# Key additions on GpSimd, tied behind the work of their own steps

## The chip, the cores and the metric

The kernel runs on one core of a Trainium2 chip. The core has five engines that run side by side and wait for each other through semaphores: TensorE (PE in the profile) multiplies matrices and writes PSUM, VectorE (DVE), ScalarE (ACT) and GpSimd (POOL) work element by element, and SyncE (SP) issues the transfers between HBM and SBUF. Each engine does its own instructions strictly in order. The metric is the device time of one execution in microseconds (us); the time before is 1137.61 us, the median of three runs (1135.73, 1138.26, 1137.61).

## What is computed

Four batches of 12480 queries attend to 49 agents, which themselves attend to 12480 keys; each output row then goes through a two-layer network with `h * cos(h)` between its layers. Cut to what matters:

```python
def sm(a, b):
    s = scale * (a @ b.transpose(0, 2, 1))
    s = s - s.max(-1, keepdims=True)
    e = np.exp(s)
    return e / (e.sum(-1, keepdims=True) + 1e-09)

agent_v = sm(agents, k) @ v            # keys: 4 x 49 x 12480
attn = sm(q, agents) @ agent_v         # queries: 4 x 12480 x 49
h = attn.reshape(49920, 128) @ w_in    # 49920 x 2048
out = (h * np.cos(h)) @ w_out          # 49920 x 128
```

## The kernel before

**The main loop.** The 49920 queries are cut into 52 groups of 960 (13 a batch, `NG`), and a group into 16 steps (`STEP`): two halves of 480 queries times eight pairs of 128 hidden units. A step `n` does three things. `first_product` (L1038) multiplies a piece of `a` (agent values already times `w_in`) by the turned query weights `pT` into a PSUM pair `ph`; ACT takes the cosine of it (`c`, L1041); `cubic_part` on DVE forms `r` from `c` and `ph` (L1047). `second_product` (L1063), four steps behind (`LAG`), multiplies `r` by `w_out`. There are 832 steps.

**The queries.** For each group the scores go through PE and are copied to a tile `e`; DVE takes the maximum (`mx`, L663) and POOL subtracts it (L665, in the burst L720). Exponentials run for whole pieces of six or seven groups at once, since ACT must change its table for them (`query_exp`, L727). Then POOL sums the exponentials of each group by a tree of additions (`query_sum`, lines L738 to L742, seven instructions a group), DVE inverts the sums (`query_inverse`, L746, L747), and for each group in turn, ten steps ahead of its use, POOL forms the weights `p` (`query_weights`, L751), PE turns them (L760), ACT copies them (L764) and POOL writes `pT` in two casts and two subtractions (`query_turned`, L767, L768).

**The keys.** While the queries of batch b - 1 are worked off, the 13 key groups of batch b are scored into a large tile `s` (`Later.scores`, L523 to L530), shifted by their maximum on POOL (`shift`, L555), exponentiated in one instruction (`exp`, L558), multiplied with the values (`values`, L492, summed on DVE at L574 and L576), and added up group by group into `es` by 12 additions on POOL (`add`, L563, one of them short). DVE reduces `es` (`total`, L581), and PE and DVE make the normalisation of it (`inverse`, L587 to L590). The first batch has another way and no such additions. Tile `s` has one buffer; its next use begins with a memset on POOL (L514).

**The burst.** Once a batch, at step 97 of its 208, `burst` puts the exponentials of the first query piece, of the keys and of the second query piece behind one another on ACT, with one change of table. There are such bursts for key batches 1, 2 and 3, at about 203, 473 and 743 us, and a last one without keys. The seven sums of the first query piece follow in the next steps; those of the second piece are planned from 16 steps behind the burst on (`lazy_sum`, L899), in a `kept_behind`.

**The order of the work.** The program is written step by step; `Plan` collects for each step which small work goes with it. The key addition of group g is planned at `plan(at + 44 + 3 * g, ab[b].add, g)` (L998), 47 to 80 steps behind the start of the burst. But what each engine really does in which order is decided by a scheduler, which may move an instruction ahead of others on its engine where no dependency forbids it. Two helpers add such dependencies, without any wait at run time: `as_traced` keeps all instructions of a stretch in their written order, and `kept_behind(engines)` ties each instruction written inside it behind the last one written before it on the same engine. It doesn't tie what comes after.

Of the kernel before, what the change touches and what calls it, by code (L numbers as in the profile page):

```python
# [46 lines left out]
def agent_attention_cos_ffn(ctx, tc, qT, kT, v, vk, vk_rest, agT, w_in, w_out, outT):  # L47
    nc = tc.nc
# [70 lines left out]
    @contextmanager  # L119
    def kept_behind(engines):  # L120

        traced = nc.cur_bb.bb.instructions
        start = len(traced)
        last = {}
        for i in reversed(traced):
            if i.engine in engines and i.engine not in last:
                last[i.engine] = i
            if len(last) == len(engines):
                break
        yield  # L130
        for i in list(traced[start:]):
            if i.engine in engines:
                tc.add_manual_dep(i, last[i.engine].name, mybir.DependencyInfo(mybir.DependencyClass.NoSync,
                                  mybir.DependencyReason.DATA), reason="kept_behind")
                last[i.engine] = i
# [121 lines left out]
    class Agents:  # L257
# [51 lines left out]
        def add(self, g):  # L309

            if g == 0:
                nc.gpsimd.tensor_copy(self.es, self.part(0))
            else:
                nc.gpsimd.tensor_add(self.es, self.es, self.part(g))
# [191 lines left out]
    class Later(First):  # L506
# [53 lines left out]
        def add(self, g):  # L560
            s = self.s[:, 8 * g:min(8 * g + 8, NT_K)]
            es = self.es[:, :s.shape[1]]
            nc.gpsimd.tensor_add(es, self.s[:, :8] if g == 1 else es, s)  # L563

        def values(self, g):
            e = self.part(g)
# [698 lines left out]
```

## Time and profile before

| | |
|---|---|
| time, median of 3 runs | 1137.61 us (1135.73 to 1138.26) |
| the profiled execution | 1132.91 us, of which 1131.0 us span |
| PE, DVE, ACT, POOL busy | 93%, 90%, 85%, 39% of the span |
| additions of the keys' exponentials, L563 | 36 on POOL |
| granted clock of TensorE, mean | 0.971 of full speed |

The page gives each engine's busy time, the chain of work that ended last with its shares by engine and line, and the costliest groups of instructions. The timeline has one line for each run of like instructions in order of time: start, length, engine, line, operation, names of the tiles written and read, count, and in brackets the idle time before it and what ended it. The table of waits adds these up by pairs of lines. POOL's share is small as a mean over the span, and its work is uneven: POOL is busy for 31.32 of the 35 us from 205 to 240 us.

### The profile page before, as it was taken

What the parts mean: (1) busy time and instruction counts of PE and PEld (TensorE: products, weight loads), DVE (VectorE), ACT (ScalarE), POOL (GpSimd) and SP (SyncE); (2) the same over time, 40 slices, a digit from 0 to 9 for tenths busy, and PEclk for the clock granted to TensorE, in tenths of its full rate; (3) what the DMA queues carried; (4) which work ended last, traced back from release to release, by engine and by line L of the source; (5) the groups of instructions that cost most, each with busy time, mean ns of one, the idle gap of its engine ahead of it and who ended that gap; (6) DMA issues with size and microseconds to landing.
All of it is one profiled execution on the core that took longest, in us unless ns stands there. A gap on an engine that the chain in (4) does not pass through costs nothing.

```text
span 1131.0 us, 30442 instructions
## 1 busy us (share of the span) xinstructions
PE 1047.6 (93%) x12759; PEld 800.4 (71%) x12759; DVE 1021.0 (90%) x1144; ACT 958.5 (85%) x1239; POOL 440.0 (39%) x733
## 2 busy tenths in 40 slices
PE   6888999869999999869999999986999999989997
PEld 2666777657877787657787777765777777766775
DVE  5859999769999999958998999986999999999997
ACT  4768888958889999868888999895898999999996
POOL 2022336784222323797313231589422223162320
PEclk9899999889999999989999999998999999989999
DMA  9733465512112245432111234441100000000001
GB/s 369 284 116 113 147 199 199 181 56 73 40 38 92 74 128 185 143 111 78 53 55 37 89 95 162 151 147 37 59 37 19 36 18 36 36 18 33 20 36 38
DMA packets 32562, 108.58 MB, mean 96 GB/s; under 512 B 3616, under 2 KB 4896, under 8 KB 32416
## 3 DMA queue, kind: packets, MB, share of 16 engines
q1 hardware_dynamic: 32416, 106.55, 27.6%
q8 instruction: 102, 1.67, 0.6%
q14 instruction: 44, 0.36, 0.1%
HBM read 80.97 MB, written 25.56 MB: 94 GB/s over the span
## 4 chain that ended last, share of the span: by engine, by line
PE 46%; DVE 30%; POOL 12%; ACT 7%; issue 4%; DMA 0%; SPq 0%; ACTq 0%; POOLq 0%; DVEq 0%
DVE r L1047 26%; PE ph L1038 19%; PE one L1063 16%; ACT c L1041 4%; POOL s L555 3%; POOL es L563 3%; POOL tree L738 3%; PE one L492 2%; PE one L523 1%; PE one L169 1%; PE one L1059 1%; PE one L1060 1%; PE ph L492 1%; PE one L760 1%; ACT e L727 1%
## 5 line engine op out<-in xcount | busy, mean ns | idle before, releaser
L1047 DVE SCALAR_TENSOR_TENSOR r<-c,ph 128x960 fp32r<-128x960 f32 x832 | 909.2, 1148 | 60.7 <-ACT c L1041 58.4
L1041 ACT ACTIVATE c<-ph 128x960 f32<-128x960 f32 x832 | 790.2, 980 | 128.6 <-PE ph L1038 105.6
L1038 PE MATMUL ph<-pT,a 113*128 113x480 f32 x1664 | 538.3, 404 | 44.1 <-POOL pT L768 29.2
L1063 PE MATMUL one<-r,w 128*128 128x480 f32 x1664 | 505.3, 390 | 0.9 <-issue 0.5
L1038 PEld LDWEIGHTS ph<-pT,a 113*128 113x128 f32 x1664 | 288.4, 190 | 167.5 <-DVE r L1047 75.2
L1063 PEld LDWEIGHTS one<-r,w 128*128 128x128 f32 x1664 | 310.8, 191 | 51.4 <-DVE r L1047 1.4
L751 POOL TENSOR_TENSOR p<-e,rz 126x392 f32<-126x392 f32 x51 | 43.1, 847 | 386.1 <-PE one L760 334.5
L768 POOL TENSOR_TENSOR pT<-p,pT 49x480 fp32r<-49x480 f32 x102 | 124.5, 1221 | 7.8
L767 POOL CAST pT<-p 49x480 fp32r<-49x480 f32 x102 | 59.4, 582 | 61.9 <-ACT p L764 57.1
L665 POOL TENSOR_TENSOR e<-e,mx 126x392 f32<-126x392 f32 x43 | 36.4, 846 | 94.7 <-DVE mx L663 94.1
L1070 ACT COPY osb<-one 128x480 f32<-128x480 f32 x80 | 44.4, 555 | 2.3 <-PE one L1063 2.2
L492 PEld LDWEIGHTS one<-s,vt 128*32 128x32 f32 (+1 forms) x2352 | 31.8, 117 | 20.3 <-issue 11.1
L169 PEld LDWEIGHTS one<-ag,xt 128*32 128x32 f32 x2752 | 33.5, 110 | 16.8 <-issue 15.1
L492 PE MATMUL one<-s,vt 128*32 128x49 f32 (+1 forms) x2352 | 37.8, 218 | 8.0 <-ACT s L558 6.8
L738 POOL TENSOR_TENSOR tree<-tree 126x96 f32<-126x96 f32 x132 | 40.1, 304 | 8.6
L169 PE MATMUL one<-ag,xt 128*32 128x49 f32 x2752 | 39.7, 210 | 2.3 <-issue 2.3
L555 POOL TENSOR_TENSOR s<-s,mxb 128x392 f32<-128x392 f32 (+1 forms) x39 | 34.4, 927 | 17.1 <-DVE mxb L551 17.1
L1059 PE MATMUL one<-pT,b 113*128 113x480 f32 x104 | 40.5, 389 | 0.0
L1060 PE MATMUL one<-pT,b 113*128 113x480 f32 x104 | 39.8, 383 | 0.0
L523 PEld LDWEIGHTS one<-ag,xt 128*32 128x32 f32 x2340 | 28.4, 110 | 15.2 <-issue 7.7
L523 PE MATMUL one<-ag,xt 128*32 128x49 f32 x2340 | 33.8, 209 | 1.9 <-DVE s L527 1.9
L563 POOL TENSOR_TENSOR es<-es,s 128x392 f32<-128x392 f32 (+1 forms) x33 | 32.4, 982 | 0.0
(160 smaller groups left out, 643.5 us busy)
## 6 DMA issues: line engine op xcount, KB each, us to landing
outT<-osb SPq DMA_DIRECT2D x51, 480.0 KB, 2.7
xt<-qT SPq DMA_DIRECT2D x49, 480.0 KB, 4.0
xt<-kT SPq DMA_DIRECT2D x43, 512.0 KB, 3.7
vt<-vk SPq DMA_DIRECT2D x42, 512.0 KB, 4.5
c<-kT SPq DMA_DIRECT2D x5, 512.0 KB, 7.6
vt<-w_in SPq DMA_DIRECT2D x8, 256.0 KB, 6.9
vt<-w_out SPq DMA_DIRECT2D x8, 256.0 KB, 7.5
c<-vk SPq DMA_DIRECT2D x3, 512.0 KB, 7.4
```

What stands on the lines that cost most here:

```text
L169: mm = nc.tensor.matmul(out[at:at + n], xt[:, t * TT + lo:t * TT + lo + n], ag, start=True, stop=True)
L492: mm = nc.tensor.matmul(po[rows], vt[:, x, rows], e, start=(first and x == 0), stop=(last and x + 1 == len(es)))
L523: mm = nc.tensor.matmul(ps[j * QS:(j + 1) * QS, t], xt[:, t * w + j * QS:t * w + (j + 1) * QS], ag[:, self.b, :], start=True, stop=True)
L555: nc.gpsimd.tensor_sub(s, s, self.mxb.unsqueeze(1).to_broadcast(list(s.shape)))
L563: nc.gpsimd.tensor_add(es, self.s[:, :8] if g == 1 else es, s)
L738: nc.gpsimd.tensor_add(t[:, :, :w], src[:, :, :w], src[:, :, w:2 * w])
L767: nc.gpsimd.tensor_copy(pT[own, c], p[own])
L768: nc.gpsimd.tensor_sub(pT[other, c], p[own], pT[own, c].bitcast(F32))
L1038: nc.tensor.matmul(ph[:, j, :CH], ai[:, f], pTs[q % 3][:, c], start=True, stop=True)
L1041: nc.scalar.activation(cos, h, AF.Sin, bias=HALF_PI, scale=1.0)
L1047: nc.vector.scalar_tensor_tensor(r, cos, 1.0, h, op0=ALU.subtract, op1=ALU.mult)
L1063: nc.tensor.matmul(po, w1[:, f, :], r[:, j, :], start=(f == 0), stop=(f == NF - 1))
```

## The change

Each key addition is now written inside a `kept_behind` for GpSimd, so that the scheduler can't move it ahead of what was written before it on that engine.

```diff
         def add(self, g):
             s = self.s[:, 8 * g:min(8 * g + 8, NT_K)]
             es = self.es[:, :s.shape[1]]
-            nc.gpsimd.tensor_add(es, self.s[:, :8] if g == 1 else es, s)
+            with kept_behind([nc.gpsimd.engine]):
+                nc.gpsimd.tensor_add(es, self.s[:, :8] if g == 1 else es, s)
```

The order of the other engines stays the same. Lines behind L563 have a number higher by one in the changed program. In the order before, POOL's rows at the end of the fourth and in the fifth sum of the first burst read so (`tree` and `rz2` are the sums of the queries, `es` and `s` those of the keys):

```order
95 L738 TENSOR_TENSOR tree_3552<-tree_3552 126x8x6
96 L563 TENSOR_TENSOR es_1489<-s_1487 128x392
97 L738 TENSOR_TENSOR tree_3552<-tree_3552 126x8x3
98 L563 TENSOR_TENSOR es_1489<-es_1489,s_1487 128x392
99 L740 TENSOR_TENSOR rz2_1785<-tree_3552 126x8
100 L563 TENSOR_TENSOR es_1489<-es_1489,s_1487 128x392
101 L741 TENSOR_TENSOR rz2_1785<-rz2_1785,tree_3552 126x8
102 L563 TENSOR_TENSOR es_1489<-es_1489,s_1487 128x392
103 L742 TENSOR_TENSOR rz2_1785<-rz2_1785,e_1784 126x8
104 L738 TENSOR_TENSOR tree_3560<-e_1784 126x192
105 L563 TENSOR_TENSOR es_1489<-es_1489,s_1487 128x392
```

The additions stand one by one between the steps of the sums, twelve of them from the fourth sum to the sixth. In the order of the change the same place reads:

```order
95 L739 TENSOR_TENSOR tree_3552<-tree_3552 126x8x6
96 L739 TENSOR_TENSOR tree_3552<-tree_3552 126x8x3
97 L741 TENSOR_TENSOR rz2_1785<-tree_3552 126x8
98 L742 TENSOR_TENSOR rz2_1785<-rz2_1785,tree_3552 126x8
99 L743 TENSOR_TENSOR rz2_1785<-rz2_1785,e_1784 126x8
100 L739 TENSOR_TENSOR tree_3560<-e_1784 126x192
```

The sums follow one another with nothing between them. The additions stand further on, in the order of the change, on POOL between the query groups that come some 40 to 80 steps behind the burst (`p` are weights, `pT` the turned ones, `e` with `mx2` a query subtraction):

```order
174 L666 TENSOR_TENSOR e_3321<-e_3321,mx2_4303 126x392
175 L564 TENSOR_TENSOR es_1489<-s_1487 128x392
176 L564 TENSOR_TENSOR es_1489<-es_1489,s_1487 128x392 x2
177 L752 TENSOR_TENSOR p_0_104<-e_1784,rz2_1785 126x2x4x49
178 L768 CAST pT_1_99<-p_4465 49x480 x2
179 L769 TENSOR_TENSOR pT_1_99<-p_4465,pT_1_99 49x480 x2
180 L564 TENSOR_TENSOR es_1489<-es_1489,s_1487 128x392 x6
181 L752 TENSOR_TENSOR p_1_105<-e_1784,rz2_1785 126x2x4x49
182 L768 CAST pT_2_100<-p_4745 49x480 x2
183 L769 TENSOR_TENSOR pT_2_100<-p_4745,pT_2_100 49x480 x2
184 L564 TENSOR_TENSOR es_1489<-es_1489,s_1487 128x392
185 L666 TENSOR_TENSOR e_3321<-e_3321,mx2_4828 126x392
```

Two more follow behind that, ahead of the memset of `s`. In the order before, the same weights, casts and subtractions stand there without the additions. The second batch has the same pattern; the third has three, six and three additions, each lot behind a `pT`.

## Rows read from the trace of the kernel before

**Rows 1.** The page: busy time by engine; the chain's shares, by engine and line.

```profile
PE 1047.6 (93%) x12759; PEld 800.4 (71%) x12759; DVE 1021.0 (90%) x1144; ACT 958.5 (85%) x1239; POOL 440.0 (39%) x733
...
PE 46%; DVE 30%; POOL 12%; ACT 7%; issue 4%; DMA 0%; SPq 0%; ACTq 0%; POOLq 0%; DVEq 0%
DVE r L1047 26%; PE ph L1038 19%; PE one L1063 16%; ACT c L1041 4%; POOL s L555 3%; POOL es L563 3%; POOL tree L738 3%; PE one L492 2%; PE one L523 1%; PE one L169 1%; PE one L1059 1%; PE one L1060 1%; PE ph L492 1%; PE one L760 1%; ACT e L727 1%
```

**Rows 2.** Who waited for whom, PE: total us, times, longest us.

```profile
PE ph L1038 <- POOL pT L768: 29.2, 5, 9.6
```

**Rows 3.** Timeline of PE: start, us, engine, line, operation, count, idle before.

```profile
239.50 1.17 PE L1038 MATMUL ph<-pT,a 113*128 113x480 f32 x2 [8.45 <-POOL pT L768]
...
509.14 1.17 PE L1038 MATMUL ph<-pT,a 113*128 113x480 f32 x2 [9.63 <-POOL pT L768]
...
528.73 0.60 PE L1038 MATMUL ph<-pT,a 113*128 113x480 f32 x2
...
778.83 1.17 PE L1038 MATMUL ph<-pT,a 113*128 113x480 f32 x2 [9.64 <-POOL pT L768]
```

**Rows 4.** Timeline of POOL, burst one.

```profile
207.13 0.61 POOL L738 TENSOR_TENSOR tree<-e 126x192 f32<-126x192 f32 x1 [0.40 <-ACT e L727]
...
209.69 0.60 POOL L738 TENSOR_TENSOR tree<-e 126x192 f32<-126x192 f32 x1
...
216.95 0.61 POOL L738 TENSOR_TENSOR tree<-e 126x192 f32<-126x192 f32 x1
...
218.34 1.03 POOL L563 TENSOR_TENSOR es<-s 128x392 f32<-128x392 f32 x1
...
236.96 1.22 POOL L767 CAST pT<-p 49x480 fp32r<-49x480 f32 x2
```

**Rows 5.** Timeline of DVE, behind the three stalls.

```profile
241.71 1.15 DVE L1047 SCALAR_TENSOR_TENSOR r<-c,ph 128x960 fp32r<-128x960 f32 x1 [8.71 <-ACT c L1041]
243.94 1.15 DVE L1047 SCALAR_TENSOR_TENSOR r<-c,ph 128x960 fp32r<-128x960 f32 x1 [1.07 <-ACT c L1041]
...
511.35 1.16 DVE L1047 SCALAR_TENSOR_TENSOR r<-c,ph 128x960 fp32r<-128x960 f32 x1 [9.87 <-ACT c L1041]
513.58 1.15 DVE L1047 SCALAR_TENSOR_TENSOR r<-c,ph 128x960 fp32r<-128x960 f32 x1 [1.08 <-ACT c L1041]
...
781.03 1.15 DVE L1047 SCALAR_TENSOR_TENSOR r<-c,ph 128x960 fp32r<-128x960 f32 x1 [9.89 <-ACT c L1041]
```

**Rows 6.** Timeline of POOL, burst two.

```profile
488.06 0.21 POOL L741 TENSOR_TENSOR rz<-rz,tree 126x8 f32<-126x8 f32 x1
...
489.95 0.85 POOL L665 TENSOR_TENSOR e<-e,mx 126x392 f32<-126x392 f32 x1
...
506.60 1.22 POOL L767 CAST pT<-p 49x480 fp32r<-49x480 f32 x2
...
525.10 2.52 POOL L768 TENSOR_TENSOR pT<-p,pT 49x480 fp32r<-49x480 f32 x2
```

**Rows 7.** Timeline of POOL, the groups behind burst one.

```profile
289.24 0.84 POOL L751 TENSOR_TENSOR p<-e,rz 126x392 f32<-126x392 f32 x1 [10.26 <-PE one L760]
...
307.63 0.84 POOL L751 TENSOR_TENSOR p<-e,rz 126x392 f32<-126x392 f32 x1 [13.57 <-PE one L760]
...
314.67 0.84 POOL L665 TENSOR_TENSOR e<-e,mx 126x392 f32<-126x392 f32 x1 [2.27 <-DVE mx L663]
324.61 0.18 POOL L514 MEMSET s<- 32x98 f32 x1 [9.09 <-PE one L492]
```

**Rows 8.** Timeline of DVE: beside additions, beside `pT`, and with neither.

```profile
222.65 7.62 DVE L1047 SCALAR_TENSOR_TENSOR r<-c,ph 128x960 fp32r<-128x960 f32 x7 [0.46 <-ACT c L1041]
...
274.21 0.88 DVE L746 TENSOR_SCALAR rz<-rz 126x48 f32<-126x48 f32 x1
...
333.08 0.84 DVE L581 TENSOR_REDUCE es<-es 128x49 f32<-128x392 f32 x1
...
364.77 5.44 DVE L1047 SCALAR_TENSOR_TENSOR r<-c,ph 128x960 fp32r<-128x960 f32 x5
```

## The prediction

> **What bounds the kernel now.** I read the page first: PE is busy for 93% of the span, DVE for 90%, GpSimd (POOL) for only 39% [rows 1]. An engine at 39% should not set the end, but the chain of waits holds 12% of POOL's work, and by line 3% of it is the key additions (L563) and 3% the sums between which they stand (L738). Twelve per cent of a chain by an engine that mostly idles says that POOL bounds a few short stretches. The table of who waited for whom then finds them: PE's first products (L1038) waited 29.2 us for `pT` of L768, in five waits, the longest 9.6 us [rows 2]. PE's timeline shows that three of them make up nearly all: 8.45, 9.63 and 9.64 us, ending at 239.50, 509.14 and 778.83 us [rows 3], together 27.72. These lie in the three bursts that hold a key exponential.
>
> POOL's timeline of the first such stretch tells why `pT` is late. From 207.13 us on POOL does the seven sums of the first query piece one after another (one sum alone takes 209.69 - 207.13 = 2.56 us), and from 218.34 us on twelve key additions of about 1.03 us stand between their steps; only behind all that comes the cast with which `pT` begins, at 236.96 [rows 4]. PE starts 2.54 us after that. POOL doesn't idle between the first sum and `pT`, so whatever stands in that row of work ahead of `pT` is on the path.
>
> DVE is what would otherwise run on: it has `r` to do without a break up to the stall, sits idle for 8.71 us, and then for 1.07 us once more, since PE restarts at a low pace: its pair of first products at 239.50 takes 1.17 us, one at 528.73 takes 0.60 [rows 3, 5]. In the second burst that is 9.87 + 1.08, and the third repeats the second (9.89). DVE's loss is 9.78 + 10.95 + 10.97 = 31.7 us. Outside such gaps it sets the pace: 26% of the chain is L1047 [rows 1].
>
> **The change, part by part.** Nothing is added or removed; PE, DVE, ACT and SP keep their order, and no DMA moves. On POOL the 12 additions of each of the three key batches leave the row of sums and go into the query groups that follow: three ahead of a `p`, six ahead of the next, one ahead of a query subtraction and two ahead of a memset (third batch: three, six, three).
>
> First, what leaves the path. Additions between the steps of a sum also fill the gaps between dependent steps, so twelve times 1.03 would be too much. I build the row anew from sums of 2.55 us. Burst one: the fourth sum starts at 216.95, ahead of every addition. Four sums from there end at 216.95 + 4 x 2.55 = 227.15 instead of 236.96, 9.81 us earlier [rows 4]. PE can use `pT` 2.54 us later, at 229.69; it has finished what it had at 239.50 - 8.45 = 231.05. So the wait goes entirely, with 1.36 us to spare.
>
> Burst two: the additions begin in the fourth sum, behind its step at 488.06. The 0.45 us left of that sum, three more sums and the one query subtraction among them (0.85) give 488.06 + 0.45 + 7.65 + 0.85 = 497.01 instead of 506.60 [rows 6]. `pT` is ready 2.54 us later, at 499.55; PE needs it at 509.14 - 9.63 = 499.51. This is a dead heat, and the third burst repeats it: the wait shrinks to some 0.04 us, and POOL is next in line there. PE then has no slow restart, and DVE goes on from one `r` to the next. I price the gain by DVE, 31.7 us, less 0.4 us a burst for an ordinary hand-off gap before `r` (0.46 us stands before the one at 222.65 [rows 8]): 30.5 us. The lower end, by PE's waits alone, is 27.7 us; the upper end is 31.7.
>
> Second, what is late next. The `pT` behind burst two has its first half at 525.10 + 1.24 = 526.34 and is first used at 528.73 [rows 3, 6]: 2.4 us to spare. POOL gets there 9.6 us earlier and PE up to 10.9, so 1.1 us are left; I cost it at nothing.
>
> Third, the additions at their new places, 11 x 1.04 + 0.4 = 11.8 us a batch. Three (3.1 us) stand ahead of the weights `p` at 289.24, before which POOL idles 10.26 us for PE; six (6.2 us) ahead of the one at 307.63, with 13.57 idle; one ahead of the subtraction at 314.67 (2.27 idle), two (1.5 us) ahead of the memset at 324.61 (9.09 idle) [rows 7]. Nobody queued behind them is due before these idle times end. The one who waits for the result is DVE's reduction at 333.08 [rows 8], 16 us behind the place of the last addition, and the next batch's scores overwrite `s` only behind that memset. I cost all this at nothing. If the cover were gone, six additions would hold one `p` up by 6.2 us.
>
> Fourth, DVE beside the moved additions. While POOL was adding, seven `r` took 7.62 us, 1.089 each; in a stretch with no additions five took 5.44, 1.088 [rows 8]. So the additions cost `r` nothing. The scaling of `rz` (L746) took 0.88 us at 274.21, while POOL was in a `pT` subtraction; if it falls beside an addition instead, it can wait for 1 us, in two places a batch, at most 6 us in all and likely none: it is short, and the additions stand in groups. The Trainium skill speaks against the change here: SBUF — State Buffer, "SBUF: two separate sides", has VectorE and GpSimd share a port pair under an exclusive lock that is held for a whole instruction, where VectorE's instruction has two SBUF inputs or runs in a two-port mode. The trace agrees for `rz`, all in SBUF, with its 0.88 us; `r` takes `c` from SBUF and `ph` from PSUM, and its 1.089 us shows no lock. Were it to hold for `r` too, the sum would turn over: the third rival.
>
> Sum: the profiled execution took 1132.91 us (span 1131.0 and 1.9 around it), 4.7 below the median of the three runs. 1132.9 - 30.5 = 1102.4; on the median 1137.6 - 30.5 = **1107.1 us**.
>
> **The rivals.** One: another wait for POOL takes part of the place of the removed one, in the dead heat of bursts two and three, or at a `p` or `pT` behind them. For it speaks that POOL's work has no idle time from the first sum to that second `pT`; against it, margins of 1.4 and 1.1 us besides the dead heat. At 3 us in each burst the gain is 30.5 - 9 = 21.5 us, and the time 1116.1.
>
> Two: the time is given back, because something was hidden behind the stall: a transfer, or ACT, at 85%. If nothing of the gain stays, the time is 1137.6. Against it: DMA has 0% of the chain, ACT 7% [rows 1], and every start behind the stalls hangs on PE, DVE or POOL.
>
> Three, slower: each addition blocks DVE for its own length at its new place. Before, some of it ran beside DVE's stall; afterwards all of it would run beside a DVE that sets the pace. Price: 3 x 11.8 = 35.4 us against a gain of 30.5, 4.9 us slower, 1142.5. It decides from 30.5 / 36 = 0.85 us an addition on. Against it: the seven `r` at 222.65 took 1.089 us each beside six additions.
>
> Four: the additions stay where they were, since a scheduler orders POOL. The order of the changed program excludes it.
>
> **How the numbers follow.** A measurement of this kernel tells about 0.2% (2.3 us) from no change. Forecast (a gain of 26 to 33 us): 0.74. Rival one (10 to 26 us): 0.20. Rival two: 0.03. Rival three: 0.03. The likeliest case's own range is 1104 to 1112. The whole range goes from the upper bound of the gain and the spread of the runs shown (2.5 us), 1102, to where rival one has most of its chance behind it, 1118. Faster 0.94, the same 0.03, slower 0.03.
>
> **What would show it.** Right: PE's waits for `pT` at L1038 fall from 29.2 us to under 4; no addition stands between sums; POOL's idle time before `p` (L751) falls by the additions' length where they now stand; DVE's idle time before `r` falls by about 30 us and its busy time stays. Wrong: a wait of PE on L768 of over 2 us behind a burst (rival one), DVE's idle time turning up behind other releasers (two), or `r` over 1.15 us beside additions (three).

## The result, and the profile after

The changed kernel takes 1105.07 us (median of 4 runs, 1103.62 to 1106.56) against 1137.93 us of the kernel before in the same measurement: a ratio of 0.9711, 95% interval 0.9687 to 0.9735. That is 32.9 us less (30.2 to 35.6). The forecast was 30.5 us less, 1107.1 us.

The page of the changed kernel, with its rows of busy time and of the chain's shares by engine, as in [rows 1], then the groups of `r` and of `p` (busy, mean ns, idle before, releaser). Line numbers behind L563 are higher by one.

```profile
span 1103.1 us, 30433 instructions
...
PE 1043.6 (95%) x12759; PEld 797.0 (72%) x12759; DVE 1020.5 (93%) x1144; ACT 958.8 (87%) x1239; POOL 444.2 (40%) x733
...
PE 52%; DVE 31%; ACT 8%; issue 4%; POOL 3%; DMA 1%; SPq 0%; ACTq 0%; POOLq 0%; DVEq 0%
...
L1048 DVE SCALAR_TENSOR_TENSOR r<-c,ph 128x960 fp32r<-128x960 f32 x832 | 908.9, 1149 | 31.3 <-ACT c L1042 29.2
...
L752 POOL TENSOR_TENSOR p<-e,rz 126x392 f32<-126x392 f32 x51 | 43.1, 847 | 351.9 <-PE one L761 300.1
```

The same two groups on the page of the kernel before:

```profile
L1047 DVE SCALAR_TENSOR_TENSOR r<-c,ph 128x960 fp32r<-128x960 f32 x832 | 909.2, 1148 | 60.7 <-ACT c L1041 58.4
...
L751 POOL TENSOR_TENSOR p<-e,rz 126x392 f32<-126x392 f32 x51 | 43.1, 847 | 386.1 <-PE one L760 334.5
```

The engines' work is the same to 1% (PE 1047.6 and 1043.6 us, POOL 440.0 and 444.2), and what changed is nearly all idle time. TensorE's mean granted clock rose from 0.971 to 0.985 of full speed. DVE's idle time before `r` fell by 29.4 us. POOL's idle time before `p` fell by 34.2 us. Thirty of the 36 additions stand ahead of a `p` now, and by their rows they take some 32 us: they fill time in which POOL waited for PE. What the other 2 us are was not traced. POOL's share of the chain fell from 12% to 3%.

The table of who waited for whom on PE, after; the first row answers to [rows 2]:

```profile
PE ph L1039 <- POOL pT L769: 1.6, 2, 0.8
```

The 27.7 us at the three bursts are gone. The two waits that are left, 0.80 and 0.77 us, come some 2.6 us ahead of the second and third burst, where the kernel before has 0.71 and 0.75. POOL's timeline of burst one, after, answers to [rows 4], and the PE row behind it to [rows 3]:

```profile
210.69 0.61 POOL L739 TENSOR_TENSOR tree<-e 126x192 f32<-126x192 f32 x1 [0.39 <-ACT e L728]
...
220.55 0.60 POOL L739 TENSOR_TENSOR tree<-e 126x192 f32<-126x192 f32 x1
...
230.80 1.23 POOL L768 CAST pT<-p 49x480 fp32r<-49x480 f32 x2
232.11 2.52 POOL L769 TENSOR_TENSOR pT<-p,pT 49x480 fp32r<-49x480 f32 x2
```

```profile
234.82 0.60 PE L1039 MATMUL ph<-pT,a 113*128 113x480 f32 x2
```

The row of seven sums takes 230.80 - 210.69 = 20.11 us instead of 236.96 - 207.13 = 29.83. `pT` is ready at 232.11 + 1.24 = 233.35, and PE takes it up at 234.82 with no idle time and at its full pace: 0.60 us a pair. DVE's timeline there goes on without the gap of [rows 5]:

```profile
226.62 7.57 DVE L1048 SCALAR_TENSOR_TENSOR r<-c,ph 128x960 fp32r<-128x960 f32 x7 [0.76 <-ACT c L1042]
234.11 0.56 DVE L664 TENSOR_REDUCE mx<-e 126x8 f32<-126x392 f32 x1
234.72 4.35 DVE L1048 SCALAR_TENSOR_TENSOR r<-c,ph 128x960 fp32r<-128x960 f32 x4
```

To compare kernels stretch by stretch I use a mark that each burst has: the start of ACT's table load ahead of the query exponentials. Before, and after:

```profile
203.26 1.28 ACT L727 ACT_TABLE_LOAD   x1
472.95 1.28 ACT L727 ACT_TABLE_LOAD   x1
742.63 1.28 ACT L727 ACT_TABLE_LOAD   x1
998.09 1.28 ACT L727 ACT_TABLE_LOAD   x1
```

```profile
206.83 1.28 ACT L728 ACT_TABLE_LOAD   x1
466.98 1.28 ACT L728 ACT_TABLE_LOAD   x1
726.60 1.28 ACT L728 ACT_TABLE_LOAD   x1
971.13 1.28 ACT L728 ACT_TABLE_LOAD   x1
```

The differences of these marks, for these two kernels and for all that follow but one (each from its own profiled execution, the median beside it from its timed runs, all in us):

| kernel | to burst 1 | 1 to 2 | 2 to 3 | 3 to last | last to end | median |
|---|---|---|---|---|---|---|
| before | 203.3 | 269.7 | 269.7 | 255.5 | 132.9 | 1137.9 |
| before, again | 209.9 | 270.4 | 270.0 | 255.8 | 133.3 | 1139.1 |
| changed | 206.8 | 260.2 | 259.6 | 244.5 | 132.0 | 1105.1 |
| changed, again | 207.2 | 259.4 | 258.9 | 245.1 | 132.4 | 1104.2 |
| batch 1 tied alone | 207.6 | 260.3 | 269.6 | 255.5 | 133.2 | 1125.3 |
| batch 3 tied alone | 208.9 | 270.1 | 269.9 | 246.3 | 132.8 | 1127.4 |
| three stay | 209.2 | 261.2 | 262.5 | 246.9 | 133.2 | 1114.7 |
| eight stay | 206.2 | 267.4 | 266.9 | 252.5 | 132.1 | 1127.3 |
| early, tied | 209.3 | 269.9 | 269.8 | 255.7 | 134.1 | 1137.0 |
| additions twice | 205.6 | 260.1 | 258.6 | 244.4 | 132.1 | 1104.5 |
| left out, scaled | 206.5 | 258.8 | 259.5 | 245.4 | 132.4 | 1104.1 |
| six sums | 204.5 | 259.6 | 259.6 | 244.3 | 132.1 | 1103.7 |

By the means of the two profiles each, the change takes 10.2, 10.6 and 10.8 us out of the three stretches that begin with a burst with keys, 31.6 together, and 0.9 us out of what lies behind the last burst. The stretch up to the first burst differs by up to 6.7 us between executions of one and the same kernel, and is looked at below.

### The profile page after: what moved, and what is told of

It is laid out like the page before. It is cut to its first block, busy times and chain, and to the rows that moved or that the text cites. A ratio compares the mean times of both kernels' runs of the same rounds, so it can differ in the third digit from the quotient of the medians.

```text
span 1103.1 us, 30433 instructions
## 1 busy us (share of the span) xinstructions
PE 1043.6 (95%) x12759; PEld 797.0 (72%) x12759; DVE 1020.5 (93%) x1144; ACT 958.8 (87%) x1239; POOL 444.2 (40%) x733
## 4 chain that ended last, share of the span: by engine, by line
PE 52%; DVE 31%; ACT 8%; issue 4%; POOL 3%; DMA 1%; SPq 0%; ACTq 0%; POOLq 0%; DVEq 0%
DVE r L1048 27%; PE ph L1039 21%; PE one L1064 18%; ACT c L1042 4%; PE one L492 3%; POOL s L555 2%; PE one L169 2%; PE one L523 2%; PE one L1060 1%; PE one L1061 1%; ACT s L558 1%; PE one L761 1%; PE ph L492 1%; PE one L374 1%; DVE run L530 1%
## 5 line engine op out<-in xcount | busy, mean ns | idle before, releaser
L769 POOL TENSOR_TENSOR pT<-p,pT 49x480 fp32r<-49x480 f32 x102 | 124.8, 1224 | 7.8
L169 PEld LDWEIGHTS one<-ag,xt 128*32 128x32 f32 x2752 | 32.9, 109 | 17.4 <-issue 15.7
L523 PE MATMUL one<-ag,xt 128*32 128x49 f32 x2340 | 34.2, 209 | 3.5 <-DVE s L527 1.9
```

Of the source, the lines that this page charges most:

```text
L169: mm = nc.tensor.matmul(out[at:at + n], xt[:, t * TT + lo:t * TT + lo + n], ag, start=True, stop=True)
L523: mm = nc.tensor.matmul(ps[j * QS:(j + 1) * QS, t], xt[:, t * w + j * QS:t * w + (j + 1) * QS], ag[:, self.b, :], start=True, stop=True)
L769: nc.gpsimd.tensor_sub(pT[other, c], p[own], pT[own, c].bitcast(F32))
```

## The experiments

**The changed kernel again**, as a mark on the same chip as the runs beside it.

> The changed kernel again, beside the others on the same chip: about 1105 us, 31 to 33 us below the kernel before. It is the mark for the runs beside it.

1104.21 us, ratio 0.9711 (0.9682 to 0.974). The result repeats.

**One batch alone.** Does each burst count by itself? Only the condition of the tie changes, `self.b == 1` and in a second kernel `self.b == 3`:

```diff
-            nc.gpsimd.tensor_add(es, self.s[:, :8] if g == 1 else es, s)
+            with kept_behind([nc.gpsimd.engine] if self.b == 1 else []):
+                nc.gpsimd.tensor_add(es, self.s[:, :8] if g == 1 else es, s)
```

> Only the additions of key batch 1 are tied; those of batches 2 and 3 stay between the sums. If the gain is the wait for pT in each burst by itself, PE's wait at the first burst (8.45 us) goes, the other two stay at 9.6 us each, and the time falls by 9.8 us against before (DVE's loss there). If the gain hangs on the order as a whole or on one later burst, it is near 0 or near 31 us.

> Only the additions of key batch 3 are tied. If each burst counts by itself, PE's waits of 8.45 and 9.63 us stay, the third goes, and the time falls by 10.9 us against before. If it hangs on the order as a whole, near 0 or near 31 us.

Batch 1 alone: ratio 0.9894 (0.9875 to 0.9913), 11.4 us faster by the medians. Its first stretch is the changed kernel's (260.3), the others are those of before (269.6, 255.5). Batch 3 alone: 0.9915 (0.9897 to 0.9933), 9.3 us; only its third stretch shrinks, by 9.3 us. The expected 9.8 and 10.9 us lie within the intervals (9.9 to 14.2 and 7.6 to 11.7) or at their edge. The gain is made burst by burst. The third stretch of batch 3 alone is still 1.5 us longer than the mean of the changed kernel's two; why is open.

**How much row, how much wait.** With `g > 3` as the condition, three additions of each batch stay between the sums; with `g > 6`, eight do (two tied ones follow the last loose one ahead, since the tie only says behind what they stand).

> In each burst three of the twelve additions stay between the sums and nine are tied behind. One addition in that row is worth (29.83 - 20.11) / 11.35 = 0.86 us, so pT is 2.6 us later than in the changed kernel, where it had 1.5, 1.1 and 0 us to spare: waits of about 1.1, 1.5 and 2.6 us, 5 us (4 to 7) above the changed kernel. If the wait had its own cause and the additions only filled it, the time stays that of the changed kernel.

> In each burst eight of the twelve additions stay between the sums and four go behind. By 0.86 us an addition pT is 6.9 us later than in the changed kernel; less the 1.5, 1.1 and 0 us to spare that is 5.4 + 5.8 + 6.9 = 18 us, and up to 1 us a burst for PE's slow restart: 18 to 21 us above the changed kernel. If the additions only filled a wait of another cause, no change against it.

PE's timeline at the three bursts, with three additions in the row, then with eight:

```profile
238.29 0.71 PE L1039 MATMUL ph<-pT,a 113*128 113x480 f32 x2 [0.79 <-POOL pT L769]
...
499.51 0.71 PE L1039 MATMUL ph<-pT,a 113*128 113x480 f32 x2 [2.13 <-POOL pT L769]
...
761.96 0.70 PE L1039 MATMUL ph<-pT,a 113*128 113x480 f32 x2 [1.94 <-POOL pT L769]
```

```profile
239.65 1.17 PE L1039 MATMUL ph<-pT,a 113*128 113x480 f32 x2 [6.87 <-POOL pT L769]
...
507.04 1.17 PE L1039 MATMUL ph<-pT,a 113*128 113x480 f32 x2 [6.21 <-POOL pT L769]
...
773.93 1.17 PE L1039 MATMUL ph<-pT,a 113*128 113x480 f32 x2 [6.83 <-POOL pT L769]
```

The ratios are 0.981 (0.9793 to 0.9827) and 0.9914 (0.9895 to 0.9933). The waits are 4.9 us and 19.9 us together; 5.2 and 18.1 had been worked out. Burst by burst the working does less well: with three, 0.79, 2.13 and 1.94 us against 1.1, 1.5 and 2.6, so that the close sum is in part luck; with eight, 6.87, 6.21 and 6.83 against 5.4, 5.8 and 6.9. Over the three stretches the loss against the changed kernel is 1.4 + 3.2 + 2.0 = 6.7 us with three, and 7.6 + 7.6 + 7.7 = 23.0 us with eight (sums of unrounded terms). In the medians it is 10.4 us (1114.65 against 1104.21) and 23.1 us, so with three it is above the 4 to 7 expected; of the 3.7 us between, the stretch up to the first burst and the one behind the last hold some 3 us in the profiles, where no addition was moved. All four timed runs lie above 1114 us (1114.26 to 1116.21), and one profile can't tell whether that is chance; it stays open. With eight it is 2 us above the range: the waits are 1.8 us longer than worked out, and the 3 us that the stretches lose beyond the waits are what the range had allowed for the slow restart. Behind a wait of 6 to 7 us PE restarts at 1.17 us a pair, behind one of 1 to 2 us at 0.70. The rows of the windows there, at the first burst, with eight additions and then with three, give TensorE's granted clock in the third figure from the end:

```profile
239.65:241.15 1.50, 1.50 (x4) 1.29 (x5) 0.00 (x0) 0.30 (x1) 1.40 (x2) 0.50 0.00 0
...
238.29:239.50 1.21, 1.21 (x6) 1.06 (x7) 1.16 (x2) 0.47 (x1) 1.19 (x1) 1.00 0.05 20
```

The slow restart is one at 0.50 of full speed, the 1.2 GHz level, behind 6.87 us of idle time; behind 0.79 us the clock was at its full 2.4 GHz. Zero, three, eight and twelve additions in the row cost 0, 6.7, 23.0 and 31.6 us. From one to the next that is 0.7, 1.1 and 0.7 us an addition and burst: the first three use up what there is to spare, and one of the last four is short.

**What the additions cost at their new place.** First all but two of a batch are left out, then, in another kernel, each is done twice.

> As the changed kernel, but of the twelve additions of a batch only the first and the last are done; ten of twelve key groups are missing from the sum. If the moved additions cost nothing at their new place, the time is that of the changed kernel within 1 us. If each blocks DVE for its own length there, it is faster by up to 30 x 1.04 = 31 us.

This kernel took 8442.95 us and says nothing on the question. With about a sixth of the sum, the normalised agent values are some six times too large, and so are the `a` made of them. By the source they then exceed the bound that the program checks at its end, and it went on through the general path that it keeps for that case; the row of its windows from there on (length, then busy times of PE, PE's loads, DVE, ACT and POOL, granted clock, DMA share, GB/s):

```profile
1100.00:8441.00 7341.00, 4235.68 (x11084) 2796.43 (x11084) 5935.56 (x6424) 2002.51 (x2156) 105.74 (x110) 0.57 0.05 14
```

So it was done again with the sum scaled up, at no further instruction:

```diff
-                nc.gpsimd.tensor_add(es, self.s[:, :8] if g == 1 else es, s)
+                if g in (1, 12):
+                    nc.gpsimd.tensor_add(es, self.s[:, :8] if g == 1 else es, s)
...
-            nc.vector.tensor_scalar_add(self.rz, pa[:KR, :1], EPS)
+            nc.vector.tensor_scalar(self.rz, pa[:KR, :1], 6.0, EPS, op0=ALU.mult, op1=ALU.add)
```

> The changed kernel with ten of the twelve additions of each batch left out (ten key groups are missing from the sum, which is multiplied by 6 in the step that already adds a constant, so that the usual path of the program is taken). If the moved additions cost nothing, the stretches between bursts stay at 259 to 260 us and the time within 1.5 us of the changed kernel. If each held up DVE, 30 x 1.04 = 31 us faster.

1104.09 us, ratio 0.9699 (0.9673 to 0.9725); the stretches are those of the changed kernel to 1 us. And twice:

```diff
                 nc.gpsimd.tensor_add(es, self.s[:, :8] if g == 1 else es, s)
+                nc.gpsimd.tensor_add(self.spare[:, :s.shape[1]], self.s[:, :8] if g == 1 else self.spare[:, :s.shape[1]], s)
```

> As the changed kernel, with a second addition of the same size into an unused tile behind each one: 24 a batch on GpSimd, at the new places. If the idle time there covers them (12.5 us of twelve against 13.57, the tightest), the time rises by 0 to 3 us. If they block DVE, by 35 us.

1104.46 us, 0.9708 (0.9685 to 0.9732). POOL's timeline at the place of the six additions, the most that stand together, in the changed kernel, then the end of it with twelve additions there instead of six:

```profile
283.21 0.85 POOL L752 TENSOR_TENSOR p<-e,rz 126x392 f32<-126x392 f32 x1 [7.03 <-PE one L761]
...
288.11 6.61 POOL L564 TENSOR_TENSOR es<-es,s 128x392 f32<-128x392 f32 x6
301.54 0.85 POOL L752 TENSOR_TENSOR p<-e,rz 126x392 f32<-126x392 f32 x1 [6.82 <-PE one L761]
```

```profile
300.27 0.85 POOL L754 TENSOR_TENSOR p<-e,rz 126x392 f32<-126x392 f32 x1 [1.41 <-PE one L763]
```

The idle time of 13.57 us before this `p` [rows 7] shrank to 6.82 and, with twelve, to 1.41. Ahead of the query subtraction, where one addition stands, it did run out: 2.27 us before, 1.07 in the changed kernel, none to speak of with two additions (the second ends at 307.23, the subtraction starts at 307.30). That cost no time either, since the subtraction starts 101.7 us behind the mark of burst one in both kernels. Neither 30 additions fewer nor 36 more move the time: from the first burst to the end it takes 896.1 and 895.3 us, in the changed kernel 896.3 and 895.9. At the new place they cost nothing that shows.

**The tie or the place?** The same tie, but the additions planned 18 steps behind the burst:

```diff
-                plan(at + 44 + 3 * g, ab[b].add, g)
+                plan(at + 18, ab[b].add, g)
```

> As the changed kernel, tied in the same way, but planned 18 steps behind the burst instead of 47 to 80. The additions then stand behind the first pT and two sums of the second piece, ahead of the next weights p. If it is the place in GpSimd's row that counts, PE now waits there for p and then for the second pT, some 10 us a burst, and the gain is nearly gone: 25 to 33 us above the changed kernel. If the tie behind the sums alone makes the gain, the time stays that of the changed kernel.

1136.95 us, ratio 0.9988 (0.9976 to 0.9999): the gain is gone, and all three stretches are those of before. The first `pT` comes in time, but ten additions now stand ahead of the next `p`. POOL's row, and PE's, at burst one:

```profile
244.22 9.80 POOL L564 TENSOR_TENSOR es<-es,s 128x392 f32<-128x392 f32 x9
253.98 0.84 POOL L752 TENSOR_TENSOR p<-e,rz 126x392 f32<-126x392 f32 x1
```

```profile
254.88 1.18 PE L761 MATMUL one<-ident,p 126*113 126x126 f32 x4 [6.66 <-POOL p L752]
```

The table of waits adds it up:

```profile
PE one L761 <- POOL p L752: 21.3, 3, 8.0
PE ph L1039 <- POOL pT L769: 4.6, 5, 1.1
```

PE waits 21.3 us for `p` in the three bursts, and some 3 us more than the changed kernel for `pT`, at burst one for the second. DVE's gap is 8.05 us there. The tie alone is worth nothing; what counts is that the additions stand where POOL has nothing pressing behind them. The kernel before is the other half of this: there the additions were planned at the late place without a tie, and the scheduler moved them ahead.

**Is POOL still what the burst waits for?** One of the seven sums is cut to a single short addition in each burst:

```diff
             e, rz = e_of[n], rz_of[n].unsqueeze(2)
+            if n in [x[0][-1] for x in pieces[:NB - 1]]:
+                nc.gpsimd.tensor_add(rz, e[:, :, 0:1], e[:, :, 1:2])
+                return
```

> The changed kernel with the sum of one query group in each of the three bursts cut to a single short addition (that group's sum is incomplete), so that the row ahead of pT is 2.3 us shorter. If PE's and DVE's own work sets the pace once the key additions are gone, the time falls by at most 1 us in all. If GpSimd's row is still what the burst waits for, by 2 us a burst, 6 us in all.

1103.65 us, ratio 0.9704 (0.9682 to 0.9726). At burst one the row takes 226.01 - 208.33 = 17.68 us, 2.43 less than in the changed kernel. From the first burst to the end the kernel takes 895.6 us, the changed kernel 896.3 and 895.9. A shorter row gains nothing more, so POOL's row no longer sets the pace; by the chain's shares (52% and 31%) it is PE and DVE that do.

**The kernel before, profiled once more**, for the stretch up to the first burst.

> The kernel before, profiled once more: about 1137 us. From one burst to the next it should take 269.7 us again; its first 203 us, up to the first burst, are expected to come out up to 5 us longer than in the first profile, since all the other kernels show 206 to 209 there.

1139.11 us, ratio 1.0007. The stretches between bursts repeat to 0.7 us, and the first came out 6.7 us longer, at the top of what the other kernels show.

## Why the prediction was right

*The bound.* Right: the three waits of PE for `pT`, with the slow restart behind each, were what the change removed, each by its own burst, as the kernels with one batch tied show.

*What leaves the path.* Right in its working. Burst one: 9.81 us earlier was worked out, and the row shrank by 29.83 - 20.11 = 9.72. PE's spare time there was put at 1.36 us and is 234.82 - 233.35 = 1.47. Burst three was called a dead heat; POOL's and PE's rows there, after:

```profile
751.89 2.53 POOL L769 TENSOR_TENSOR pT<-p,pT 49x480 fp32r<-49x480 f32 x2
```

```profile
753.17 0.70 PE L1039 MATMUL ph<-pT,a 113*128 113x480 f32 x2
```

Ready at 751.89 + 1.24 = 753.13, used at 753.17. Burst two:

```profile
492.25 2.53 POOL L769 TENSOR_TENSOR pT<-p,pT 49x480 fp32r<-49x480 f32 x2
...
494.56 0.60 PE L1039 MATMUL ph<-pT,a 113*128 113x480 f32 x2
```

Ready at 493.49, used at 494.56: PE came about 1 us later behind the mark than worked out, so there was room. That it erred to this side was luck, since the dead heat left none.

*The price.* DVE's loss as the measure was right; whether the 0.4 us a burst taken off it was right can't be told. At the place of the former gap in burst one DVE has no idle time (the `mx` at 234.11 and the `r` at 234.72), which speaks against the deduction. The three stretches give 31.6 us by the means, close to DVE's 31.7 without it; but the two profiles whose rows are shown give 9.5 + 10.1 + 10.9 = 30.5, the two later ones 32.7. What the median has beyond 31.6 is 1.3 us, within its interval; 0.9 us of it is behind the last burst in the profiles, and why is open.

*What is late next.* Right: no wait of PE for the second `pT` appeared. The early variant shows what lies beyond the room there: additions ahead of that stretch cost all that the change gains.

*The new places.* Right: they cost nothing that shows, and as much again costs nothing either.

*DVE beside the additions.* Right. Beside the six additions at 288.11 four `r` take 4.34 us, 1.085 each, against 1.089 and 1.088 in [rows 8]:

```profile
289.70 4.34 DVE L1048 SCALAR_TENSOR_TENSOR r<-c,ph 128x960 fp32r<-128x960 f32 x4
```

So the exclusive port lock of the Trainium skill (SBUF — State Buffer, "SBUF: two separate sides") leaves `r` alone here, as its condition says for an instruction with at most one input in SBUF, outside the two-port modes. The scaling of `rz` took 0.88 us again, at 268.18, beside a `pT` subtraction as before, and each time it ends 0.04 us behind the pair of subtractions (269.06 and 269.02, before 275.09 and 275.05). The scalings of the first pieces, beside the short steps of the sums, took 0.18 to 0.32 us. The third rival, 4.9 us slower, falls with the kernel that adds everything twice: 36 more additions, no change. Rival one did not come up: no wait of PE on L769 behind a burst is left. Of rival two nothing is seen: the gain of each stretch stays to the end.

## What to carry to other kernels

An engine that is busy for 40% can still set the time of a stretch, if a scheduler fills its row with work that is ready but not urgent just where something urgent queues up behind: look at the chain's share of an idle engine, then at what stands in its row ahead of the tile that is waited for. Such work is to be tied to where it may be late, and it takes both, the place and the tie: planned at 47 to 80 steps behind the burst without a tie it was moved ahead, tied at 18 steps it gained nothing, tied at 47 to 80 steps it gained all. Price a shortened row by the idle time of the engine that would run on, and count interleaved instructions at what they add to the row, not at their own length.

## What the runs showed of the hardware that was not expected

An addition that stands between the steps of a sum lengthens the row by less than it takes: twelve of them, 11 x 1.03 + 0.4 = 11.7 us of work, lengthened it by 9.72 us, and six in a row, each needing the one before, take 6.61 us, 1.10 each. POOL's rows before, two steps of a sum with nothing between them, then two with an addition between:

```profile
209.24 0.21 POOL L741 TENSOR_TENSOR rz<-rz,tree 126x8 f32<-126x8 f32 x1
209.53 0.20 POOL L742 TENSOR_TENSOR rz<-rz,e 126x8 f32<-126x8 f32 x1
...
220.52 0.20 POOL L740 TENSOR_TENSOR rz<-tree 126x8 f32<-126x8 f32 x1
220.68 1.03 POOL L563 TENSOR_TENSOR es<-es,s 128x392 f32<-128x392 f32 x1
221.67 0.20 POOL L741 TENSOR_TENSOR rz<-rz,tree 126x8 f32<-126x8 f32 x1
```

The dependent step starts 0.08 us after the end of the one before it; the addition, which needs neither, starts 0.04 us ahead of that end. Small dependent steps on POOL have gaps that other work fills.

The program up to the first burst is the same in all these kernels, and took from 203.3 to 209.9 us. The windows of the first 100 us, for the kernel before in its two profiles, columns as above:

```profile
0.00:100.00 100.00, 79.60 (x1685) 55.93 (x1686) 69.35 (x130) 66.71 (x152) 16.78 (x40) 0.95 0.66 238
```

```profile
0.00:100.00 100.00, 77.89 (x1551) 54.36 (x1551) 66.43 (x126) 62.16 (x148) 16.78 (x40) 0.91 0.63 228
```

TensorE's mean granted clock there was 0.95 of full speed in the faster execution and 0.91 in the slower, and the loads came in at 238 and 228 GB/s. Which of the two leads wasn't tried. Over all twelve profiles in the table the clock alone doesn't order the times: with 0.97 in these windows the first stretch took 204.5 to 207.6 us, with 0.95 it took 203.3 to 207.2. For a change of 2% it is enough to move a comparison of two single executions by 0.6%; the stretches between marks don't suffer from it.
